# Dealing the hidden columns of a fused attention and feed-forward kernel to partitions in runs of four

## The chip, the cores and the metric

The kernel runs on one core of a Trainium2 chip. A core has a matrix engine (TensorE, PE in the profile, with its weight loads shown apart as PEld), VectorE (DVE), ScalarE (ACT), GpSimd (POOL), SyncE (SP), and 16 DMA engines that all queues share. Partitions are the 128 rows of the on-chip memory. The metric is device time in microseconds (us), lower is better. Before the change the median of three runs is 367.38 us (366.16 to 367.57).

## The reference

Attention over 8 batches, 8 heads, 576 positions and a head dimension of 64: each position sees the positions at most 32 away, and 8 global positions see and are seen by all. Then, over all 4608 tokens, a feed-forward layer with 2048 hidden columns and a periodic activation:

```python
scores = scale * np.matmul(q, k.transpose(0, 1, 3, 2))
mask = np.abs(pos[:, None] - pos[None, :]) <= window
mask = mask | is_global[:, None] | is_global[None, :]
...
h = x @ w_in
s = np.sin(alpha * h)
g = h + s * s / (alpha + 1e-09)
return (g @ w_out).astype(np.float32)
```

w_in is 512 x 2048, w_out 2048 x 512, alpha has 2048 values, all float32. A hidden column belongs to one column of w_in, one value of alpha and one row of w_out; in which order the 2048 are worked off makes no difference to the sum.

## The kernel before

The program is one function with an order written out by hand: each engine does its instructions in the order in which the code issues them, and a DMA waits in the queue of the engine that issues it. The phases alternate over the 8 batches: `phase_a(b + 1, b)` is attention of batch b + 1, with the second matrix product of batch b strewn between its steps (`gemm2` is a generator, and `fill(n)` issues n of its matmuls); `gemm1(b)` is the first product with the activation.

**Attention.** `attention(b)` goes over four head pairs `hp`. `scores` makes blocks of keys by queries in PSUM (line 742), ACT takes the exponential (750), DVE multiplies with the mask (753). One head pair later `products` multiplies with the values in `VX` and with ones for the denominators (784). PE is in order: in batch 1 the first `products(0, ...)` stands behind two groups of scores of head pair 1 and ahead of the third. `warm` (546) issues matmuls without a use.

`VX[b % 2]` holds a batch's values. `load_v` (394) fetches them with POOL's DMAs, 16 of 36 KB a batch. The rows of the global positions come by `load_vg` (403): 8 DMAs of SP, one a head, each of 8 x 12 runs of 64 bf16. For batch 1 and on they are copied out of `VGb`, which `cast_globals_v` (696) makes on POOL from `gv`, and `gv` is gathered by SP (489).

**First product.** `gemm1` goes over 16 groups `nt` of 128 hidden columns. The columns of a group lie on the 128 partitions of the result, so alpha and its reciprocal are one value a partition, held in `alphaT` and `recipT` (128 x 16). Eight matmuls a group (line 992) each load a 128 x 128 block of w_in as weights and stream 288 or 320 tokens. ACT takes the sine (1022), ACT or DVE squares it (1026, 1028), DVE adds (1030) into `H2`.

**Second product.** `gemm2` takes blocks of 128 tokens of `H2` as weights and streams `w_out[:, nt, :]`, 512 columns, over the 16 groups (1049). Partition p of group nt of `w_out` must hold the row of the hidden column that lies there in `H2`. ACT copies the result out (1055), and SP writes it (1062).

**Loads of the parameters.** All go through POOL's queue, which casts float32 to bf16 on the way. `load_w_in` (411) is called for the quarters 0 and 1 between the loads of batch 0's values, and for 2 and 3 once batch 1's transposed keys have landed. `load_w_out` (417) is called in `gemm1(0)` at group 11 and issues four DMAs of 128 x 4 runs of 512 floats. Behind it in POOL's order stand `cast_globals_v`, `place_globals(1)` (372 and 377, copies of the global keys and queries into `KX` and `QX`, from `kTg` and `qTg`, which DVE makes at 708), and the second half of batch 1's `load_v`; then `load_vg(1)` on SP.

**alpha.** SP loads it as 16 rows of 128 into `arow` (483), behind six small loads of the global positions and ahead of eight register loads (485) and the gathers. PE transposes `arow` (680) into a PSUM tile, and ACT copies that to `alphaT` (684), behind its placing of the global keys and queries of batch 0. DVE makes `recipT` at the start of attention 0 (1119).

**The tail.** Column norms of w_in (897, a matmul of one column for each of 16 groups, weights taken from `W2`), token norms, `judge`, and `gemm2_globals` (1076) with a scatter by POOL (1083). `judge` gives a verdict that every engine reads (1081); the branch at 1206 would run `general_path` if the inputs were out of bounds, which they are not. Between the two, PE issues 54 matmuls (1199) whose results nothing reads.

Of the kernel before, what the change touches and what calls it, by code (L numbers as in the profile page):

```python
# [12 lines left out]
DT = mybir.dt  # L13
# [3 lines left out]
P = 128  # L17
# [3 lines left out]
WCOL = 120  # L21
# [5 lines left out]
QROW = QLEN + 2 * PAD  # L27
CUT = 3 * SEG
PLACES = [(w, t, y) for w in (1, 0) for t in range(2) for y in range(2)]
LIM_SUM = float(2.0**50)  # L30
LIM_REC = float(2.0**40)
TINY = float(2.0**-60)
LIM_ARG2 = 9.3


def general_path(tc, q, k, v, global_idx, out, w_in, w_out, alphaT, recipT):


    nc = tc.nc
    B, H, S, D = q.shape  # L40
    NKT = S // KW
    NT = alphaT.shape[1]
    CT = w_in.shape[1]
    DM = w_out.shape[2]
    HALF = S // 2
# [3 lines left out]
    hi = float(np.float32(6.28125))  # L49
# [4 lines left out]
    with ExitStack() as gx:  # L54
# [4 lines left out]
        idf = one.tile([P, P], DT.float32, name="g_idf")  # L59
# [5 lines left out]
            out=g64[:],  # L65
# [14 lines left out]
        for j in range(NG):  # L80
            for at, acc in ((pos, colg), (row, rowg)):
                nc.vector.scalar_tensor_tensor(
                    out=acc[:], in0=at[:], scalar=gf[:, j : j + 1], in1=acc[:],
# [23 lines left out]
        with tc.For_i(0, B, 1) as b:  # L107
# [87 lines left out]
            for nt in range(NT):  # L195
                hg = ps.tile([P, 2, 512], DT.float32, name="g_pt")
                for c in range(CT):
                    for e in range(2):
                        nc.tensor.matmul(
                            out=hg[:, e, 0:HALF], lhsT=w_in[:, c, nt * P : (nt + 1) * P],  # L200
                            rhs=xT[:, c, e * HALF : (e + 1) * HALF],
                            start=(c == 0), stop=(c == CT - 1),
                        )
                y = wk.tile([P, 2, HALF], DT.float32, name="g_y")
                n = wk.tile([P, 2, HALF], DT.float32, name="g_n")
                nc.vector.tensor_scalar(
                    out=y[:], in0=hg[:, :, 0:HALF], scalar1=alphaT[:, nt : nt + 1], scalar2=None,
                    op0=ALU.mult,
                )
                nc.vector.tensor_scalar(  # L210
                    out=n[:], in0=y[:], scalar1=1.0 / TWO_PI, scalar2=None, op0=ALU.mult
                )
                for m in (MAGIC, -MAGIC):
                    nc.vector.tensor_scalar(out=n[:], in0=n[:], scalar1=m, scalar2=None, op0=ALU.add)
                for part in (hi, mid, low):
                    nc.vector.scalar_tensor_tensor(
                        out=y[:], in0=n[:], scalar=-part, in1=y[:], op0=ALU.mult, op1=ALU.add
                    )
                edge = float(np.nextafter(np.float32(np.pi), np.float32(0)))
                nc.vector.tensor_scalar(  # L220
                    out=y[:], in0=y[:], scalar1=edge, scalar2=-edge, op0=ALU.min, op1=ALU.max
                )
                nc.scalar.activation(out=y[:], in_=y[:], func=AF.Sin)
                nc.vector.tensor_tensor(out=y[:], in0=y[:], in1=y[:], op=ALU.mult)
                nc.vector.scalar_tensor_tensor(
                    out=HB[:, nt, :].rearrange("p (e c) -> p e c", e=2),
                    in0=y[:], scalar=recipT[:, nt : nt + 1], in1=hg[:, :, 0:HALF],
                    op0=ALU.mult, op1=ALU.add,
                )
# [18 lines left out]
def kernel(  # L248
# [11 lines left out]
    nc = tc.nc  # L260
# [144 lines left out]
                in_=src[:, None, :].to_broadcast([NG, NT12, D]),  # L405
            )

    def load_w_in(gs):
        for g in gs:
            cols = slice(g * DFF // 4, (g + 1) * DFF // 4)  # L410
            nc.gpsimd.dma_start(
                out=w_in[:, :, cols], in_=moe_w_in[:, cols].rearrange("(c p) n -> p c n", p=P)
            )

    def load_w_out():
        for g in range(4):
            nc.gpsimd.dma_start(
                out=w_out[:, 4 * g : 4 * g + 4, :],
                in_=moe_w_out[4 * g * P : (4 * g + 4) * P, :].rearrange("(t p) n -> p t n", p=P),
            )  # L420


# [49 lines left out]
        out=g64[:],  # L472
        in_=bass.AP(tensor=global_idx.tensor, offset=global_idx.offset, ap=[[1, NG], [0, B], [1, 1]]),
    )
    arow = setup.tile([NT, P], DT.float32, name="arow")
    nc.sync.dma_start(out=girow[:], in_=global_idx[None, :])
    for t in (0, D):
        nc.sync.dma_start(out=gp64[t + KT : t + KT + NG], in_=global_idx[:, None])
# [1 line left out]
            out=gidx8[t + KT : t + KT + NG],  # L480
            in_=bass.AP(tensor=global_idx.tensor, offset=global_idx.offset, ap=[[0, NG], [1, NG]]),
        )
    nc.sync.dma_start(out=arow[:], in_=moe_alpha.rearrange("(t p) -> t p", p=P))
    gi32 = girow[:].bitcast(DT.int32)
    greg = [nc.sync.value_load(gi32[0:1, 2 * j : 2 * j + 1], min_val=0, max_val=S - 1) for j in range(NG)]

# [71 lines left out]
    nc.scalar.activation(out=qrel[:], in_=qrel[:], func=AF.Square, bias=kpos[:, 0:1], scale=-1.0)  # L558
    clear(vflat[:, half : 2 * half])
    load_v(0, (0,))  # L560
    load_w_in((0,))
    load_v(0, (1, 2))
    load_w_in((1,))
    load_v(0, (3,))
    cast_qk(1)
    load_vg(0)
# [108 lines left out]
    for w, name in ((1, "k"), (0, "q")):  # L675
# [1 line left out]
        nc.tensor.transpose(  # L677
            out=pg[w][:], in_=g0[name][:], identity=identb[0 : NG * B, 0 : NG * B]
        )
    nc.tensor.transpose(out=both[:, 0:NT], in_=arow[:], identity=idf[0:NT, 0:NT])  # L680
    for t in range(2):
        place_global_keys(t, act)
        place_global_queries(t, act)
    act(out=alphaT[:], in_=both[:, 0:NT])
    turn_part(0, 1, views([z[:] for z in zo]))
    turn_part(1, 1, views([zn[:, n, :] for n in range(2)]))
    def second_half():
# [206 lines left out]
    def column_norms(pw):  # L894

        for nt in range(NT):
            nc.tensor.matmul(
                out=pw[:, nt : nt + 1], lhsT=W2[:, nt * P : (nt + 1) * P], rhs=ones[:, 0:1],
                start=True, stop=True, skip_group_check=True,
            )  # L900
        c2 = normp.tile([P, NT], DT.float32, name="c2")
        nc.vector.tensor_tensor(out=c2[:], in0=alphaT[:], in1=alphaT[:], op=ALU.mult)
        nc.vector.tensor_tensor(out=c2[:], in0=pw[:, 0:NT], in1=c2[:], op=ALU.mult)
        nc.vector.tensor_reduce(out=limit[:], in_=c2[:], axis=AX.X, op=ALU.max)
        nc.vector.tensor_scalar(
            out=limit[:], in0=limit[:], scalar1=1e-30, scalar2=1.0 / LIM_ARG2, op0=ALU.max, op1=ALU.mult
        )
        nc.vector.reciprocal(out=limit[:], in_=limit[:])
# [60 lines left out]
    def gemm1(b):  # L969
# [11 lines left out]
        def chunks(nt, cs):  # L981
            if nt not in hs:
                if order[nt] == "o":
                    hs[nt] = [(slice(e, e + 1), zo[e][:, None, :]) for e in range(2)]
                else:
                    h = {"n": zn, "d": zd}.get(order[nt]) or hr.tile([P, 2, 512], DT.float32, name="zr")
                    hs[nt] = [(slice(0, 2), h[:])]
            h = [ap[:, i] for es, ap in hs[nt] for i in range(es.stop - es.start)]
            for c in cs:
                for e in range(2):  # L990
                    lhsT = w_in[:, c, nt * P : (nt + 1) * P]
                    nc.tensor.matmul(  # L992
                        out=h[e][:, 0:W], lhsT=lhsT, rhs=xT[:, c, e, 0:W],
                        start=(c == 0), stop=(c == CT - 1), skip_group_check=True,
                    )
# [118 lines left out]
    def phase_a(b_att, b_moe):  # L1114
        def beside(at):

            if b_moe is None:
                if at == -1:
                    nc.vector.tensor_scalar(out=recipT[:], in0=alphaT[:], scalar1=1e-9, scalar2=None, op0=ALU.add)
                    nc.vector.reciprocal(out=recipT[:], in_=recipT[:])  # L1120
                if at == 0:
                    second_half()
                    nc.gpsimd.memset(VX[1][:].bitcast(DT.int32), 0)
                    nc.gpsimd.memset(QX[1][:].bitcast(DT.int32), 0)
                    nc.gpsimd.memset(KX[1][:].bitcast(DT.int32), 0)
                    turn_qk(1)
                    nc.gpsimd.tensor_copy(out=seen[:], in_=turned[1][1][0:1, 0:1])
                    load_w_in((2, 3))
                    load_v(1, (0, 1))
                    gather(v, gv)  # L1130
                return
            if 0 <= at < 2 and b_moe:
                square_x(b_moe, at)
            if b_att == 1 and at == 0:
                place_rest(1)
                place_rest(0)
            for which, t, y in places_at(b_att, at):
                place(b_att + 1, which, t, y, nc.vector.tensor_copy)
            if b_moe == 0 and at == 2:
                turn_qk(2)  # L1140

        if b_moe is not None:
            waiting.append(gemm2(b_moe))
        attention(b_att, beside)
# [46 lines left out]
    verdicts = judge(zn[:, 0, :])  # L1191
    next(verdicts)
    sure = gemm2_globals(verdicts)
    tiles = [(r, c) for r in (0, D) for c in (0, D)]
    for kinds, n in ((tiles, 6), (tiles[0:2], 6), (tiles[0::3], 6), ([None], 6)):
        for i in range(n):
            for at in kinds:
                rows, cols = (slice(0, P), slice(0, P)) if at is None else [slice(x, x + D) for x in at]
                nc.tensor.matmul(
                    out=(zn if len(kinds) == 2 else zd)[cols, (rows.start or 0) // D, 0:WCOL],  # L1200
                    lhsT=VX[0][rows, 0, i, cols], rhs=H2[rows, i, 0:WCOL],
                    start=True, stop=True, skip_group_check=True,
                )
    mctx.close()

    with tc.If(sure < P, preferred_fallthrough_block=False):  # L1206
# [31 lines left out]
```

## Time and profile before

| what | us |
|---|---|
| median of three runs | 367.38 (366.16 to 367.57) |
| the profiled execution | 366.15 |
| its span in the profile | 364.4 |
| PE busy | 338.4 |
| ACT busy | 293.5 |
| DVE busy | 283.3 |
| POOL busy | 139.2 |
| 1024 weight loads from w_in, PEld | 98.6 |
| 576 matmuls of the second product | 153.7 |

The span is what the profile covers, from the first instruction to the last; the time of the execution holds 1.75 us more. Busy times are sums over the span. Matmuls overlap in the machine and their ends are modelled, so PE's busy time is not work at full rate. Where a row ends in brackets, they hold the idle time of the engine just before it and what ended it. The DMA share of a stretch can go over 1, since an engine works at several packets at once; q0 is the queue that POOL fills, q1 the one that SP fills. The granted clock is the share of PE's full clock.

### The profile page before, as it was taken

What the parts mean: (1) busy time and instruction counts of PE and PEld (TensorE: products, weight loads), DVE (VectorE), ACT (ScalarE), POOL (GpSimd) and SP (SyncE); (2) the same over time, 40 slices, a digit from 0 to 9 for tenths busy, and PEclk for the clock granted to TensorE, in tenths of its full rate; (3) what the DMA queues carried; (4) which work ended last, traced back from release to release, by engine and by line L of the source; (5) the groups of instructions that cost most, each with busy time, mean ns of one, the idle gap of its engine ahead of it and who ended that gap; (6) DMA issues with size and microseconds to landing.
All of it is one profiled execution on the core that took longest, in us unless ns stands there. A gap on an engine that the chain in (4) does not pass through costs nothing. (4 is left out here: it accounts for less than half of the span.)

```text
span 364.4 us, 8575 instructions
## 1 busy us (share of the span) xinstructions
PE 338.4 (93%) x3110; PEld 230.8 (63%) x3110; DVE 283.3 (78%) x623; ACT 293.5 (81%) x566; POOL 139.2 (38%) x246
## 2 busy tenths in 40 slices
PE   2579978999999999999999999999999999999994
PEld 1467656766567666776666766766676766655453
DVE  6776998588988877888888887888788866798661
ACT  7689997886978788887888897979888888878711
POOL 7992686669874702661066304730000000000001
PEclk9999998999999999999999999999999999999999
DMA  7997999999999783989199904647120011000321
GB/s 118 120 171 162 181 146 189 156 168 198 146 237 202 73 123 81 172 89 161 31 158 120 149 29 50 68 50 148 43 59 29 2 31 60 29 3 0 105 70 53
DMA packets 103580, 38.07 MB, mean 104 GB/s; under 512 B 94139, under 2 KB 98251, under 8 KB 103083
## 3 DMA queue, kind: packets, MB, share of 16 engines
q0 software_dynamic: 56640, 18.56, 44.6%
q1 hardware_dynamic: 46890, 18.89, 25.5%
q8 instruction: 26, 0.43, 0.5%
q14 instruction: 24, 0.19, 0.2%
HBM read 37.15 MB, written 17.83 MB: 151 GB/s over the span
## 5 line engine op out<-in xcount | busy, mean ns | idle before, releaser
L1049 PE MATMUL zo<-w_out,H 128*128 128x512 bf16 x576 | 153.7, 379 | 0.0
L992 PEld LDWEIGHTS <-w_in 128*128 128x128 bf16 x1024 | 98.6, 98 | 45.6 <-issue 9.1
L394 POOL DMA_DIRECT2D VX<-in_v_dram x128 | 83.3, 659 | 89.8 <-PE zd L784 62.9
L1049 PEld LDWEIGHTS <-H 128*128 128x128 bf16 x576 | 52.3, 97 | 37.2
L750 ACT ACTIVATE E<-ring 128x480 bf16<-128x480 f32 x96 | 54.2, 567 | 22.6 <-PE ring L742 22.2
L753 DVE TENSOR_TENSOR E<-E,MASK 128x480 bf16<-128x480 bf16 x96 | 36.0, 405 | 16.9 <-ACT E L750 15.5
L1083 POOL DMA_INDIRECT out_dram<-osb,ghalf x1 | 1.1, 1067 | 119.6 <-POOLq L1206 119.6
L1030 DVE SCALAR_TENSOR_TENSOR H<-s,recipT,zn 128x576 bf16<-128x576 bf16 x47 | 38.2, 814 | 10.3 <-ACT s L1026 6.5
L1026 ACT ACTIVATE s<-sb 128x576 bf16<-128x576 bf16 (+1 forms) x62 | 42.7, 689 | 2.0
L742 PE MATMUL ring<-QX,KX 128*128 128x120 bf16 x384 | 38.0, 225 | 6.5 <-ACT E L750 3.0
L742 PEld LDWEIGHTS <-KX 128*128 128x128 bf16 x384 | 29.0, 102 | 22.0 <-issue 8.8
L1022 ACT ACTIVATE sb<-zn,alphaT 128x576 bf16<-128x576 f32 (+1 forms) x47 | 34.7, 739 | 9.8 <-PE zn L992 9.7
L1030 DVE SCALAR_TENSOR_TENSOR H<-s,recipT,zd 128x576 bf16<-128x576 bf16 x39 | 31.7, 814 | 6.5 <-ACT s L1026 4.7
L1030 DVE SCALAR_TENSOR_TENSOR H<-s,recipT,zr 128x576 bf16<-128x576 bf16 x39 | 31.7, 813 | 4.5 <-ACT s L1026 2.4
L1022 ACT ACTIVATE sb<-zd,alphaT 128x576 bf16<-128x576 f32 (+1 forms) x39 | 28.9, 740 | 7.1 <-PE zd L992 5.8
L1028 DVE TENSOR_TENSOR s<-sb 128x576 bf16<-128x576 bf16 (+1 forms) x66 | 30.7, 465 | 4.1 <-ACT sb L1022 3.6
L1022 ACT ACTIVATE sb<-zr,alphaT 128x576 bf16<-128x576 f32 (+1 forms) x39 | 28.9, 740 | 5.6 <-PE zr L992 5.4
L784 PEld LDWEIGHTS <-VX 128*128 128x128 bf16 x448 | 26.6, 100 | 9.4 <-issue 3.5
L1055 ACT COPY osb<-zo 128x512 f32<-128x512 f32 x36 | 20.8, 577 | 11.3 <-PE zo L1049 10.0
L992 PE MATMUL zn<-xlast,w_in 128*128 128x288 bf16 (+1 forms) x192 | 28.8, 289 | 0.3
L992 PE MATMUL zn<-xT,w_in 128*128 128x288 bf16 x184 | 26.9, 286 | 2.3 <-DVE H L1030 0.9
L784 PE MATMUL zn<-E,VX 128*128 128x120 bf16 (+2 forms) x336 | 26.9, 211 | 1.0 <-DVE xlast L816 0.9
(163 smaller groups left out, 492.6 us busy)
## 6 DMA issues: line engine op xcount, KB each, us to landing
VX<-in_v_dram POOLq DMA_DIRECT2D x128, 36.0 KB, 5.4
kd<-in_k_dram POOLq DMA_DIRECT2D x7, 576.0 KB, 7.1
qd<-in_q_dram POOLq DMA_DIRECT2D x7, 576.0 KB, 10.1
w_in<-in_moe_w_in_dram POOLq DMA_DIRECT2D x4, 512.0 KB, 6.0
w_out<-in_moe_w_out_dram POOLq DMA_DIRECT2D x4, 512.0 KB, 7.8
out_dram<-osb SPq DMA_DIRECT2D x8, 256.0 KB
out_dram<-osb SPq DMA_DIRECT2D x8, 224.0 KB
out_dram<-osb SPq DMA_DIRECT2D x8, 192.0 KB
```

Of the source, the lines that this page charges most:

```text
L394: nc.gpsimd.dma_start(out=VX[b % 2][r : r + 24, hp, :, t * D : t * D + D], in_=v[b, 2 * hp + t].rearrange("(i a y) d -> y a i d", a=24, y= ...
L742: nc.tensor.matmul(out=ps[:, e * WCOL : (e + 1) * WCOL], lhsT=kx[:, hp, i, :], rhs=qx[:, hp, :, s0 : s0 + 60], start=True, stop=True, skip ...
L750: nc.scalar.activation(out=Eg, in_=ps[:, 0 : 4 * WCOL], func=AF.Exp, scale=scale, accum_out=EA[:, n : n + 1])
L753: nc.vector.tensor_tensor(out=Eg, in0=Eg, in1=MASK[:, 4 * g : 4 * g + 4, :].rearrange("p i c -> p (i c)"), op=ALU.mult,)
L784: nc.tensor.matmul(out=out_t[:, half, :, a - half * CUT : z - half * CUT], lhsT=OB[:] if key else VXb[:, hp, i, :], rhs=E[:, i, :, a - s0 ...
L992: nc.tensor.matmul(out=h[e][:, 0:W], lhsT=lhsT, rhs=xT[:, c, e, 0:W], start=(c == 0), stop=(c == CT - 1), skip_group_check=True,)
L1022: nc.scalar.activation(out=sb[:, es, 0:W], in_=h[:, :, 0:W], func=AF.Sin, scale=alphaT[:, nt : nt + 1])
L1026: nc.scalar.activation(out=s2[:, :, 0:W], in_=sb[:, :, 0:W], func=AF.Square)
L1028: nc.vector.tensor_tensor(out=s2[:, :, 0:W], in0=sb[:, :, 0:W], in1=sb[:, :, 0:W], op=ALU.mult)
L1030: nc.vector.scalar_tensor_tensor(out=H2[:, nt, r0 : r0 + S].rearrange("p (e c) -> p e c", e=2)[:, es], in0=s2[:, es, 0:HALF], scalar=recip ...
L1049: nc.tensor.matmul(out=ops[:], lhsT=H2[:, nt, blk * P : (blk + 1) * P], rhs=w_out[:, nt, :], start=(nt == 0), stop=(nt == NT - 1),)
L1055: nc.scalar.copy(out=osb[:], in_=ops[:])
```

## The change

Hidden columns are dealt to partitions in runs of four. Before, partition p of group nt holds column 128 nt + p. After, the groups come in fours: in the g-th four, partition p of group 4g + t holds column 512 g + 4 p + t. `columns(nt)` gives these as a slice with a step of four.

* w_in lies in memory as before. Its weight blocks are read with a step of four columns, in `gemm1`, in `column_norms` (from `W2`) and in `general_path`.
* w_out is loaded with two DMAs instead of four, each of 128 x 2 runs of 2048 floats: four rows that follow each other in memory go to one partition.
* alpha goes straight into `alphaT`, with 128 x 4 runs of four floats; `arow`, PE's transpose and ACT's copy are gone.
* `load_w_in` takes bounds instead of a list. It issues the same four DMAs in the same places.
* The 54 matmuls at the end are gone.

```diff
+RUN = 4
+def columns(nt):
+    at = nt // RUN * RUN * 128 + nt % RUN
+    return slice(at, at + RUN * 127 + 1, RUN)
...
-    def load_w_in(gs):
-        for g in gs:
-            cols = slice(g * DFF // 4, (g + 1) * DFF // 4)
+    def load_w_in(lo, hi):
+        cols = slice(lo * DFF // 4, hi * DFF // 4)
+        nc.gpsimd.dma_start(
+            out=w_in[:, :, cols], in_=moe_w_in[:, cols].rearrange("(c p) n -> p c n", p=P)
+        )
+
+    def load_w_out():
+        for half in range(2):
+            rows = slice(half * DFF // 2, (half + 1) * DFF // 2)
             nc.gpsimd.dma_start(
-                out=w_in[:, :, cols], in_=moe_w_in[:, cols].rearrange("(c p) n -> p c n", p=P)
-            )
-
-    def load_w_out():
-        for g in range(4):
-            nc.gpsimd.dma_start(
-                out=w_out[:, 4 * g : 4 * g + 4, :],
-                in_=moe_w_out[4 * g * P : (4 * g + 4) * P, :].rearrange("(t p) n -> p t n", p=P),
+                out=w_out[:, half * NT // 2 : (half + 1) * NT // 2, :].rearrange("p (g t) n -> p g (t n)", t=RUN),
+                in_=moe_w_out[rows].rearrange("(g p t) n -> p g (t n)", p=P, t=RUN),
             )
...
-    arow = setup.tile([NT, P], DT.float32, name="arow")
...
-    nc.sync.dma_start(out=arow[:], in_=moe_alpha.rearrange("(t p) -> t p", p=P))
+    nc.sync.dma_start(
+        out=alphaT[:].rearrange("p (g t) -> p g t", t=RUN),
+        in_=moe_alpha.rearrange("(g p t) -> p g t", p=P, t=RUN),
+    )
...
-    nc.tensor.transpose(out=both[:, 0:NT], in_=arow[:], identity=idf[0:NT, 0:NT])
...
-    act(out=alphaT[:], in_=both[:, 0:NT])
...
-                out=pw[:, nt : nt + 1], lhsT=W2[:, nt * P : (nt + 1) * P], rhs=ones[:, 0:1],
+                out=pw[:, nt : nt + 1], lhsT=W2[:, columns(nt)], rhs=ones[:, 0:1],
...
-                    lhsT = w_in[:, c, nt * P : (nt + 1) * P]
+                    lhsT = w_in[:, c, columns(nt)]
...
-                    load_w_in((2, 3))
+                    load_w_in(2, 3)
+                    load_w_in(3, 4)
...
-    tiles = [(r, c) for r in (0, D) for c in (0, D)]
-    for kinds, n in ((tiles, 6), (tiles[0:2], 6), (tiles[0::3], 6), ([None], 6)):
...
```

More of the change, by code (lines that the diff above doesn't have):

```diff
@@ L199, in general_path @@
                         nc.tensor.matmul(
-                            out=hg[:, e, 0:HALF], lhsT=w_in[:, c, nt * P : (nt + 1) * P],
+                            out=hg[:, e, 0:HALF], lhsT=w_in[:, c, columns(nt)],
                             rhs=xT[:, c, e * HALF : (e + 1) * HALF],
@@ L560 @@
     load_v(0, (0,))
-    load_w_in((0,))
+    load_w_in(0, 1)
     load_v(0, (1, 2))
-    load_w_in((1,))
+    load_w_in(1, 2)
     load_v(0, (3,))
@@ L1193 @@
     sure = gemm2_globals(verdicts)
-    tiles = [(r, c) for r in (0, D) for c in (0, D)]
-    for kinds, n in ((tiles, 6), (tiles[0:2], 6), (tiles[0::3], 6), ([None], 6)):
[L1196 to L1203, printed above, removed]
     mctx.close()
```

## The prediction

> **What bounds the kernel now.** I read the page first: the span, the busy shares, the costliest groups.
>
> ```profile
> span 364.4 us, 8575 instructions
> PE 338.4 (93%) x3110; PEld 230.8 (63%) x3110; DVE 283.3 (78%) x623; ACT 293.5 (81%) x566; POOL 139.2 (38%) x246
> L992 PEld LDWEIGHTS <-w_in 128*128 128x128 bf16 x1024 | 98.6, 98 | 45.6 <-issue 9.1
> ```
>
> PE leads. The stretches tell where it isn't full (columns: stretch, its length, then busy time and count of PE, PEld, DVE, ACT and POOL, the granted clock, DMA share, GB/s).
>
> ```profile
> 50.00:60.00 10.00, 7.25 (x66) 5.30 (x66) 9.51 (x24) 8.30 (x19) 8.57 (x18) 0.83 1.27 195
> 100.00:150.00 50.00, 49.49 (x479) 33.84 (x478) 40.70 (x85) 41.60 (x90) 23.38 (x43) 1.00 0.92 147
> 52.30:55.70 3.40, 1.26 (x12) 0.75 (x11) 3.14 (x8) 3.34 (x7) 3.21 (x9) 1.00 1.23 193
> 55.70:59.10 3.40, 3.25 (x24) 2.41 (x24) 3.28 (x10) 2.63 (x10) 3.24 (x5) 0.50 1.34 208
> 62.50:66.00 3.50, 3.06 (x43) 2.35 (x43) 1.87 (x6) 2.45 (x8) 2.93 (x5) 1.00 1.38 201
> ```
>
> From 100 us on PE is busy 99% of the time: what is lost before is not made up, and little can be won there. Between 50 and 60 PE stands for a while, and after a stretch with 1.26 us of work in 3.4 its clock is granted at 0.50. This is exactly where w_out is loaded. The timeline of that place (start, length, engine, line, count):
>
> ```profile
> 46.85 3.08 POOL L417 DMA_DIRECT2D w_out<-in_moe_w_out_dram  x4 [0.23 <-DMA VX<-in_v_dram]
> 49.65 0.42 DVE L708 CAST kTg<-zo 128x256 bf16<-128x256 f32 x1
> 49.92 0.63 POOL L696 CAST VGb<-H 64x512 bf16<-64x512 f32 x1
> 50.48 3.13 POOL L372 COPY KX<-kTg 64x96 bf16<-64x96 bf16 x8
> 50.58 13.96 SPq L403 DMA_DIRECT2D VX<-VGb  x16
> 53.67 0.69 POOL L377 COPY QX<-qTg 128x112 bf16<-128x112 bf16 x2
> 54.42 0.37 PE L742 MATMUL ring<-QX,KX 128*128 128x120 bf16 x4 [1.96 <-POOL QX L377]
> 58.28 0.58 PE L784 MATMUL zn<-E,VX 128*128 128x88 bf16 x4
> ```
>
> Batch 1's scores wait 1.96 us for POOL, which issues w_out, then casts the global values (VGb), then places global keys and queries. The cast also releases SP's sixteen small loads into VX; the first two of them must land before PE's products at 58.28, which start without a wait of their own.
>
> **The change, part by part.** *w_out: four transfers become two.* The four issues take 3.08 us on POOL, 0.77 each; two are gone: 1.54 us. The cast behind them, and SP's load_vg(1), can start up to that much earlier: SP at 50.58 - 1.55 = 49.0. The copies L372 need kTg, ready at 49.65 + 0.42 = 50.07; they start at 50.48 now, so they win 0.35 us at most, then DVE is the late one. PE's 1.96 us wait shrinks by as much.
>
> The transfer is the harder half. Its bytes stay (2.10 MB written); its packets go from 2048 of 1 KB to 512 of 4 KB. DMA queues by stretch (q0 is POOL's, q1 SP's; after each name packets, MB, share); in order 48.4:60.5 (w_out), 26.4:30.4 (the 18 KB packets of kd and qd), 50.6:54.8, 54.8:58.2, 60.5:62:
>
> ```profile
> q0 software_dynamic: 2643, 2.14, 117.8%
> ...
> DMA packets 98, 0.80 MB, mean 200 GB/s; under 512 B 54, under 2 KB 54, under 8 KB 54
> q0 software_dynamic: 64, 0.77, 91.0%
> q1 hardware_dynamic: 32, 0.01, 1.4%
> ...
> q0 software_dynamic: 756, 0.75, 117.6%
> ...
> DMA packets 996, 0.71 MB, mean 210 GB/s; under 512 B 336, under 2 KB 996, under 8 KB 996
> q1 hardware_dynamic: 312, 0.04, 14.6%
> ...
> q1 hardware_dynamic: 407, 0.05, 39.7%
> ```
>
> Two things are read from them. First, speed: 2.14 MB in 12.1 us is 177 GB/s in 1 KB packets, 0.77 MB in 4 us is 193 in 18 KB packets. Longer packets gain 0 to 9%; w_out's 11.7 us end near 60.1 instead of 60.4 (59.3 at best). Second, how SP's small packets come through: in 50.6:54.8 none did, though SP issues from 50.58 on (that stretch has no q1 line); then, in 54.8:58.2, 312 beside 996 - 336 = 660 of 1 KB, one per 2.1. Beside 18 KB packets it is 32 to 98 - 54 = 44, one per 1.4. So the queues take turns by packets, not by bytes. Before, 2048 turns were to be had during w_out; now 512, 44 a us.
>
> The first two loads of load_vg(1) write 8 x 12 runs of 64 bf16 each (line 403): 192 packets of 128 B. They queue up from 49.0. If again nothing moves for 4.3 us (50.58 to 54.8), they start at 53.3, when about 215 of the 512 large packets are gone; the other 297 give 297 / 2.1 = 141 turns by 60.1, and the remaining 51 follow at 407 / 1.5 = 271 a us, 0.2 us: 60.3. Bounds: no waiting at first and one per 1.4 end at 49.0 + 192 * 1.4 / 44 = 55.1, in time; nothing moved until w_out is through ends at 60.4 + 0.7 = 61.1. I take 60.3, because pause and ratio come from the same two transfers in the same place, only with other packets. PE's products then start 60.3 - 58.28 = **2.0 us later** (0 to 2.8). PE is in order: batch 1's remaining scores stand behind them, ACT and DVE starve, and the 0.35 us won before is swallowed.
>
> The Trainium skill ("DMA: Bandwidth & Descriptors", section "Queues, rings and completion order") says that each DMA engine serves its queues in turn, switching at packet boundaries; it speaks against this change, and the trace agrees with its 2.1 and 1.4. Strictly one for one it would give 49.0 + 4.3 + 192 / 44 = 57.7, in time, so the ratios decide, not the rule.
>
> The clock: an idle 2 us in 3.4 was followed by 0.50 at 55.7. A second such stretch, over 62.5:66 with 3.06 us of PE work, would cost 0 to 1.5 us. I take **0.6**.
>
> *Weights with a step of four.* No row shows such a load. Contiguous ones:
>
> ```profile
> 347.05 0.54 PE L897 MATMUL zn<-ones,W 128*128 128x1 bf16 x16
> 35.56 1.14 PE L992 MATMUL zd<-xT,w_in 128*128 128x288 bf16 x8
> L992 PE MATMUL zd<-xT,w_in x152: 282/286/286, 35.6 to 290.7; 128*128 128x288 bf16 x152
> ```
>
> Sixteen loads with one-column matmuls take 0.54 us: at most 34 ns each, less than the 98 ns that a PEld row says. In gemm1 matmuls start (1.14 - 0.286) / 7 = 122 ns apart, so a load may take 3.6 times as long before PE sees it. Cost 0, the cover being the matmul before it; a load four times as long, 136 ns, costs 14 * 1024 = 14.3 us. No gain is possible, since 122 ns is the matmul's own pace. I take 0, for the cover is wide. column_norms' 16 loads lie in the tail, under 1 us either way.
>
> The Trainium skill ("TensorE: Matmul & The Clock Gate", section "Weight-path perf modes — Fast Weight Load (FWL) and DoubleRow") keeps fast loading for steps up to 1,024 elements; without it the same page gives columns / 1.2, an estimated 107 ns, still under 122. By both the sum stays.
>
> *alpha in place.* One transfer of 16 runs becomes 512 runs of 16 B; PE's transpose, ACT's copy go.
>
> ```profile
> 3.46 0.32 SPq L483 DMA_DIRECT2D arow<-in_moe_alpha_dram  x1
> 12.26 3.73 DVE L612 COPY QX<-zd 64x288 bf16<-64x288 bf16 x8
> 14.96 0.17 ACT L684 COPY alphaT<-pg 128x16 f32<-128x16 f32 x1
> 16.02 0.17 DVE L1119 TENSOR_SCALAR recipT<-alphaT 128x16 f32<-128x16 f32 x1
> 16.14 0.96 PE L742 MATMUL ring<-QX,KX 128*128 128x120 bf16 x8 [1.45 <-DVE QX L612]
> SPq L340 <- DMA H<-in_q_dram: 2.3, 1, 2.3
> ```
>
> The first scores wait for DVE (12.26 + 3.73 = 15.99), not for ACT (15.13): the 0.17 us gain nothing. On SP the value loads, the gathers, load_vg(0) and the transposes stand behind this issue; SP idles 2.3 us ahead of the transposes, so a longer issue is hidden up to that. The landing is wanted by 16.02, 12.2 us after the issue ends; at 271 a us 512 packets need 1.9 us, and turns beside the first big loads take the rest. Cost 0, up to 1.5 if it lands late.
>
> *The 54 matmuls at the end go.*
>
> ```profile
> 357.91 0.54 PE L1199 MATMUL zd<-H,VX 64*64 64x120 bf16 x24
> 359.60 1.07 POOL L1083 DMA_INDIRECT out_dram<-osb,ghalf  x1 [119.64 <-POOLq L1206]
> SPq L1233 <- DMA out_dram<-osb,ghalf: 1.4, 1, 1.4
> ```
>
> SP's last step waits 1.4 us for POOL's scatter, which reads nothing of them: 0, between -0.5 and +0.3 for the branch behind. load_w_in is called with other bounds, in the same order: 0.
>
> **Sum** against the profiled execution, 366.15 us (span 364.4 and 1.75 around it): + 2.0 + 0.6 = 368.75. The median shown, 367.38, lies 1.23 above that execution; taking half of it, **369.3 us**, 0.5% over the median. Its own range: 367.5 (1.3 us in all) to 372.
>
> **Rivals.**
> *The small loads come in time* (not slower). For it: the products start at 58.28, and without a pause one turn per 2.1 ends at 49.0 + 192 * 2.1 / 44 = 58.2, with the pause one per 1.4 at 59.4. Against it: both the pause and the 2.1 were seen beside this very transfer. It decides at a landing before 58.0. Then only the 0.35 us is left: 365.8 as profiled, 366.4 for a median; with PE's wait shorter the half clock may also stay away, worth up to 3.25 / 2 = 1.6 us: 364.8.
> *The strided weights show.* At 136 ns a load, 381.7; at 130, 8 * 1024 = 8.2 us, 375.6. For it: no row excludes it, and it hits 1024 loads. Against it: 88 ns of cover. It decides above 122 ns.
> *alpha lands late*, after about 17: DVE holds the first masks; + 0.5 to 1.5 us beside the forecast, 370.3.
>
> **How the numbers follow.** Forecast 0.52, in time 0.30 (a fifth of it with the clock kept), strided weights 0.12, alpha late 0.06. A measurement of this kernel tells about 0.5% from no change: 365.5 to 369.2. Faster: the clock kept, 0.06. Slower: 0.36 of the forecast's 0.52 (its range straddles 369.2), weights 0.12, alpha 0.05: 0.53. Same: the rest, 0.41. The range, 365.8 to 373.5, leaves out the kept clock and the worst of the weights.
>
> **What would show it.** Right: the products (L784 before) of batch 1 start near 60.3 instead of 58.28, PE's idle before them names the VX loads or nothing; SP's packets during w_out fall to about half; w_out ends near 60; POOL's two issues take 1.5 us and the first scores start near 54.1. matmuls of gemm1 stay 122 ns apart. Wrong: products at 58 or earlier (turns by bytes, or shorter packets than 4 KB); gemm1 further apart; a first wait for alpha on DVE near 16 us.

## The result, and the profile after

The changed kernel takes 380.06 us in the median (379.40 to 381.63), the kernel before 366.96 (366.16 to 367.57) beside it: a ratio of 1.036, 95% interval 1.034 to 1.039. The profiled execution took 379.65. That is 10.8 us above the forecast of 369.3, and above the top of its range.

The page of the changed kernel, busy times and the two groups of the first product:

```profile
span 378.0 us, 8417 instructions
PE 334.5 (88%) x3010; PEld 244.4 (65%) x3055; DVE 283.4 (75%) x623; ACT 293.0 (78%) x565; POOL 138.0 (37%) x244
L999 PEld LDWEIGHTS <-w_in 128*128 128x128 bf16 x1024 | 115.5, 114 | 44.2 <-issue 20.3
L999 PE MATMUL zn<-xT,w_in 128*128 128x288 bf16 x184 | 27.8, 290 | 14.9 <-DMA w_in<-in_moe_w_in_dram 12.9
```

PE has about as much to do as before (334.5 against 338.4 us), but its share of the span fell from 93% to 88%. The last row says where: 12.9 us of idle time ahead of the first product, ended by a load of w_in. The timeline of the place, changed kernel:

```profile
33.05 0.41 PE L999 MATMUL zn<-xT,w_in 128*128 128x288 bf16 x2 [0.56 <-DVE xT L823]
36.93 1.53 POOL L417 DMA_DIRECT2D w_in<-in_moe_w_in_dram  x2
46.35 1.12 PE L999 MATMUL zn<-xT,w_in 128*128 128x288 bf16 x4 [12.89 <-DMA w_in<-in_moe_w_in_dram]
47.34 1.43 POOL L424 DMA_DIRECT2D w_out<-in_moe_w_out_dram  x2 [0.19 <-issue]
49.43 0.74 ACT L1029 ACTIVATE sb<-zn,alphaT 128x576 bf16<-128x576 f32 x1 [14.48 <-PE zn L999]
```

and the same place before:

```profile
33.60 0.90 PE L992 MATMUL zn<-xT,w_in 128*128 128x288 bf16 x6 [0.56 <-DVE xT L816]
36.74 1.54 POOL L411 DMA_DIRECT2D w_in<-in_moe_w_in_dram  x2
42.68 1.15 PE L992 MATMUL zn<-xT,w_in 128*128 128x288 bf16 x8 [0.79 <-DMA w_in<-in_moe_w_in_dram]
```

Before, PE runs six matmuls of the first group and goes on; only group 8, the first of quarter 2, waits 0.79 us for the third load. After, two matmuls of the first weight block (block row c = 0) run at 33.05, and then PE stands until 46.35. It stands for the two loads that POOL issues at 36.93, which bring the quarters 2 and 3; the groups that it wants to work on lie in quarter 0, which has long been there. By the trace's records of landings the fourth load is complete at 46.22, and PE goes on 0.13 us later.

The stretches (columns as in the prediction), after:

```profile
33.20:46.30 13.10, 0.26 (x2) 0.00 (x0) 1.40 (x5) 1.73 (x3) 6.27 (x10) 0.62 1.22 182
46.30:50.10 3.80, 3.75 (x16) 2.35 (x17) 0.00 (x0) 0.67 (x2) 2.68 (x4) 0.50 1.10 82
100.00:300.00 200.00, 196.87 (x1783) 146.59 (x1813) 164.49 (x328) 170.31 (x333) 72.65 (x134) 1.00 0.68 103
```

and before:

```profile
33.60:46.30 12.70, 11.87 (x96) 8.98 (x95) 10.83 (x22) 12.21 (x21) 6.66 (x11) 1.00 1.24 196
100.00:300.00 200.00, 198.58 (x1842) 136.79 (x1841) 162.92 (x326) 169.06 (x336) 62.21 (x115) 1.00 0.62 96
```

In the 13 us in which PE did 11.87 us of work it now does 0.26, and ACT and DVE starve with it. When it goes on, its clock is granted at 0.50 for another 3.8 us. From 100 us on both kernels are full, so the loss stays.

### The profile page after: what moved, and what is told of

Its sections match the earlier page's. It is cut to its first block, busy times and chain, and to the rows that moved or that the text cites. A ratio compares the mean times of both kernels' runs of the same rounds, so it can differ in the third digit from the quotient of the medians.

```text
span 378.0 us, 8417 instructions
## 1 busy us (share of the span) xinstructions
PE 334.5 (88%) x3010; PEld 244.4 (65%) x3055; DVE 283.4 (75%) x623; ACT 293.0 (78%) x565; POOL 138.0 (37%) x244
## 5 line engine op out<-in xcount | busy, mean ns | idle before, releaser
L1056 PE MATMUL zo<-w_out,H 128*128 128x512 bf16 x531 | 143.5, 379 | 1.9
L999 PEld LDWEIGHTS <-w_in 128*128 128x128 bf16 x1024 | 115.5, 114 | 44.2 <-issue 20.3
L749 PE MATMUL ring<-QX,KX 128*128 128x120 bf16 x384 | 37.2, 221 | 7.7 <-ACT E L757 3.8
L999 PE MATMUL zn<-xT,w_in 128*128 128x288 bf16 x184 | 27.8, 290 | 14.9 <-DMA w_in<-in_moe_w_in_dram 12.9
L379 POOL COPY KX<-kTg 64x96 bf16<-64x96 bf16 x56 | 21.7, 387 | 16.2 <-DVE kTg L715 13.9
```

Of the source, the lines that this page charges most:

```text
L379: nc.gpsimd.tensor_copy(out=KX[b % 2][rows, hp, :, t * D + KT : t * D + KT + NG], in_=kTg[rows, hp, None, :, b].to_broadcast([D, NT12, NG]),)
L749: nc.tensor.matmul(out=ps[:, e * WCOL : (e + 1) * WCOL], lhsT=kx[:, hp, i, :], rhs=qx[:, hp, :, s0 : s0 + 60], start=True, stop=True, skip ...
L999: nc.tensor.matmul(out=h[e][:, 0:W], lhsT=lhsT, rhs=xT[:, c, e, 0:W], start=(c == 0), stop=(c == CT - 1), skip_group_check=True,)
L1056: nc.tensor.matmul(out=ops[:], lhsT=H2[:, nt, blk * P : (blk + 1) * P], rhs=w_out[:, nt, :], start=(nt == 0), stop=(nt == NT - 1),)
```

## The experiments

**The step alone.** The kernel before, with only the weights read with a step of four (columns of w_in then meet other values of alpha and other rows of w_out):

```diff
-                    lhsT = w_in[:, c, nt * P : (nt + 1) * P]
+                    lhsT = w_in[:, c, columns(nt)]
...
-                out=pw[:, nt : nt + 1], lhsT=W2[:, nt * P : (nt + 1) * P], rhs=ones[:, 0:1],
+                out=pw[:, nt : nt + 1], lhsT=W2[:, columns(nt)], rhs=ones[:, 0:1],
```

> The kernel before with one part of the change, the weight blocks of w_in read with a step of four (w_out, alpha and the tail as before, so columns of w_in are paired with other values of alpha and other rows of w_out: same work, another sum). Theory: a block with a step of four of block row c = 1 is taken to overlap the later quarters of w_in, whose DMAs write the columns around it, so the second weight load of the first product waits for all four loads. Then the first product stands until the last quarter lands, about 46 instead of 33.6, and the time is 367 + 13 = 380, 378 to 382. Rival, the wait comes from the other parts (two large w_out transfers or alpha crowd the queue): 366 to 368 here. Rival, part of it is the reading itself, a slower weight load: gemm1's matmuls further apart than 122 ns and more than 381.

Measured: 379.72 us, ratio 1.036 (1.032 to 1.041). The timeline:

```profile
33.36 0.41 PE L1000 MATMUL zn<-xT,w_in 128*128 128x288 bf16 x2 [0.55 <-DVE xT L824]
45.22 1.12 PE L1000 MATMUL zn<-xT,w_in 128*128 128x288 bf16 x4 [11.45 <-DMA w_in<-in_moe_w_in_dram]
```

The step alone makes the wait and the whole loss; the other parts of the change add nothing beside it that can be told. The changed kernel's records of w_out and of batch 1's attention tell why:

```profile
DMA to landing us min/median/max: 7.9/10.1/12.2
```

```profile
67.30 0.37 PE L749 MATMUL ring<-QX,KX 128*128 128x120 bf16 x4 [1.64 <-POOL QX L384]
71.13 0.36 PE L791 MATMUL zn<-E,VX 128*128 128x88 bf16 x4
```

w_out, issued at 47.34 and 48.06, has landed by 48.06 + 12.2 = 60.3 at the latest, before batch 1's first scores at 67.30 and 11 us before its products. SP's small loads do land later than before (the second at 60.61, against 57.66), but nothing waits for them any more.

**All but the step.** The changed kernel with contiguous blocks (other pairs of columns again):

```diff
 def columns(nt):
-    at = nt // RUN * RUN * 128 + nt % RUN
-    return slice(at, at + RUN * 127 + 1, RUN)
+    return slice(nt * 128, (nt + 1) * 128)
```

> The changed kernel with contiguous weight blocks again (w_out in two transfers, alpha in place, no matmuls at the end; columns of w_in are paired with other values of alpha and rows of w_out: same work, another sum). Theory: without the wait for all of w_in, what is left is the rest of the change. As predicted, SP's small loads of the global values land late beside w_out's 4 KB packets: the products of batch 1 start near 60.3 and the time is 368.5 to 370. Rival, they come in time: products at 58.3 or before, 365 to 367. Rival, the wait does not come from the step: 379 to 381.

Measured: 369.32 us, ratio 1.008 (1.005 to 1.011). In the timeline the first product doesn't stop, and the products of batch 1 start late:

```profile
32.99 0.90 PE L998 MATMUL zn<-xT,w_in 128*128 128x288 bf16 x6 [0.56 <-DVE xT L822]
60.16 0.49 PE L790 MATMUL zn<-E,VX 128*128 128x88 bf16 x4 [2.89 <-DMA VX<-in_v_dram]
```

58.28 before, 60.16 here, 60.3 forecast. The row names a load of values, but PE's own waiting instruction, which waits for the counter of SP's second small load among others, goes through at 60.06, and that counter is full at 60.03. So the second thing that the change does is the one that was predicted, and it can only be seen once the first is away.

**The step, with w_in laid out by quarters.** This is the changed kernel with one thing more. Is the wait for data that PE needs, or for a region that it is taken to touch? Each load of w_in writes four pieces, one a block row; from its first to its last element such a load reaches over most of the tile. Here the tile holds the quarters one after the other, so that each load writes one block:

```diff
-    w_in = const.tile([P, CT, DFF], DT.bfloat16, name="w_in")
+    w_in = const.tile([P, 4, CT, DFF // 4], DT.bfloat16, name="w_in")
...
-            out=w_in[:, :, cols], in_=moe_w_in[:, cols].rearrange("(c p) n -> p c n", p=P)
+            out=w_in[:, lo], in_=moe_w_in[:, cols].rearrange("(c p) n -> p c n", p=P)
...
-                    lhsT = w_in[:, c, columns(nt)]
+                    lhsT = w_in[:, nt // 4, c, nt % 4 : nt % 4 + 509 : 4]
```

> The changed kernel whole, with the tile of w_in laid out by quarters, so that each of the four loads writes one block of memory and a block with a step of four lies within one quarter. Step, transfers and sum are as in the changed kernel. Theory: the wait is one of bookkeeping and goes, and the time is that of the changed kernel with contiguous blocks, 365 to 370 within 0.3%. Rival, the step of four costs by itself: more than the contiguous one by 1% or more, matmuls of gemm1 over 122 ns apart. Rival, the wait is for the data (the transfers crowd each other): still 379 to 381.

Measured: 369.77 us, ratio 1.009 (1.005 to 1.012), against 369.32 with contiguous blocks. The timeline, and the group of weight loads (the last row of the timeline names DVE; here too PE's waiting instruction for the second small load goes through at 60.32, with the landing at 60.29):

```profile
33.55 0.90 PE L999 MATMUL zn<-xT,w_in 128*128 128x288 bf16 x6 [0.55 <-DVE xT L823]
35.50 1.14 PE L999 MATMUL zd<-xT,w_in 128*128 128x288 bf16 x8
42.51 1.17 PE L999 MATMUL zn<-xT,w_in 128*128 128x288 bf16 x8 [0.68 <-DMA w_in<-in_moe_w_in_dram]
60.43 0.36 PE L791 MATMUL zn<-E,VX 128*128 128x88 bf16 x4 [2.33 <-DVE E L760]
```

```profile
L999 PEld LDWEIGHTS <-w_in 128*128 128x128 bf16 x1024 | 114.8, 114 | 30.8 <-issue 7.1 <-DVE HG L1043 3.3 <-DMA w_in<-in_moe_w_in_dram 1.0
```

Same step, same transfers, the data land much as before (the fourth load at 45.06), and the first product runs as before, with 0.68 us of wait at group 8. The 13 us were bookkeeping: a block with a step of four was taken to touch what the loads of the later quarters write between its elements. It fits that only the block of c = 0 got through, whose columns 0 to 508 lie ahead of the first element of every later quarter. The waits that the traces record with the weight loads say the same:

```
kernel before:          first weight load of group 4 waits for load 2, of group 8 for load 3, of group 12 for load 4
changed kernel:         third weight load of group 0, the first of c = 1, waits for loads 3 and 4; none later
w_in by quarters:       as the kernel before
```

The loads 1 and 3 share one counter and 2 and 4 another; which of the two is meant follows from the times. By which rule the waits are placed is read from these three programs only. The weight loads' own record is 114 ns instead of 98, and eight matmuls still take 1.14 us.

**The layout alone.** The control: the kernel before, contiguous blocks, tile by quarters.

```diff
-                    lhsT = w_in[:, c, nt * P : (nt + 1) * P]
+                    lhsT = w_in[:, nt // 4, c, nt % 4 * P : (nt % 4 + 1) * P]
```

> The kernel before with only the tile of w_in laid out by quarters, blocks contiguous: the control for the layout. Theory: no change, 366 to 368, since waits and transfers are as before and only places in memory differ. Rival, the layout itself gains or costs (other runs written by the DMAs, the column norms' squares read in four pieces): over 0.5% from the kernel before.

Measured: 365.75 us, ratio 0.998 (0.996 to 1.000): no change that can be told.

**Packets of 1 KB, 2 KB and 4 KB.** Three kernels with the step, w_in by quarters and w_out in four transfers, which read the same rows. They differ in the places where the four rows of a partition lie in w_out's tile, and so in the runs that are written. 4 KB:

```diff
-        for half in range(2):
-            rows = slice(half * DFF // 2, (half + 1) * DFF // 2)
+        for g in range(4):
+            rows = slice(g * DFF // 4, (g + 1) * DFF // 4)
...
+                out=w_out[:, 4 * g : 4 * g + 4, :].rearrange("p t n -> p (t n)"),
+                in_=moe_w_out[rows].rearrange("(p t) n -> p (t n)", p=P),
```

> The changed kernel with w_in by quarters, and w_out in four transfers instead of two, its packets 4 KB as in the change. Against the kernel with 1 KB packets only the packets' size differs, against the changed kernel with w_in by quarters only the number of issues. Theory: products of batch 1 near 60.2, 369 to 370.5; the two more issues of POOL (1.5 us) are swallowed in that wait. Rival, the number of issues does it: 366 to 367.2.

1 KB, the rows of a partition apart (2 KB has them in pairs, `[P, 2, NT // 4, 2, DM]`):

```diff
-    w_out = const.tile([P, NT, DM], DT.bfloat16, name="w_out")
+    w_out = const.tile([P, 4, NT // 4, DM], DT.bfloat16, name="w_out")
...
+                out=w_out[:, :, g, :], in_=moe_w_out[rows].rearrange("(p t) n -> p t n", p=P)
```

> The changed kernel with w_in by quarters, and w_out in four transfers whose packets write 1 KB again: the tile of w_out holds the four rows of a partition apart, so 2048 runs of 512 bf16 are written, not 512 runs of 2048. The rows that are read, the pairing and the sum stay. Theory: the size of the packets holds up SP's small loads of the global values, so with 1 KB ones the second of them lands near 57.7 as in the kernel before, the products of batch 1 start near 58.3, and the time is 366 to 367.2. Rival, the order of issue or the rows that are read do it: products near 60.2 and 369 to 370.

> As the kernel with 1 KB packets (w_in by quarters, w_out in four transfers, same rows and same sum), with packets that write 2 KB: 1024 runs of 1024 bf16. Theory, the queues take turns by packets: the second of SP's small loads lands between the two sizes, near 58.5 to 59.3 (57.7 with 1 KB, 60.0 with 4 KB), the products of batch 1 start there, and the time is 366.3 to 368.5. Rival, there is a step in size above which SP gets no turns: 57.7 and 365.7, or 60.0 and 369.7.

Measured; the landing is that of SP's second small load, from the trace's records of its counter:

```
packets   second small load lands   products start   median us   ratio (95%)
1 KB      57.66                     58.58            365.67      0.999 (0.998 to 1.001)
2 KB      59.47                     59.60            367.01      1.003 (1.000 to 1.005)
4 KB      60.02                     60.16            369.71      1.010 (1.007 to 1.012)
before    57.66                     58.28
```

One further execution with 4 KB took 1943 us, for a reason that no trace here shows. It is one of the five behind the median of 369.71; the other four lie between 368.83 and 369.88, with 369.55 in the middle. PE's waiting instruction for the second small load goes through at 60.05 with 4 KB and at 59.50 with 2 KB, 0.03 us after the landing in both. In the waits of the 4 KB and of the 2 KB kernel the small loads are named (who waited for what; us, times, longest):

```profile
PE zn L791 <- DMA VX<-VGb: 2.6, 1, 2.6
```

```profile
PE zn L791 <- DMA VX<-VGb: 1.0, 1, 1.0
```

The queues in 54.8:58.2, with 1 KB, 2 KB and 4 KB (under 512 B are the small ones, q1 is SP's):

```profile
DMA packets 990, 0.72 MB, mean 211 GB/s; under 512 B 327, under 2 KB 990, under 8 KB 990
...
q1 hardware_dynamic: 308, 0.04, 14.4%
```

```profile
DMA packets 535, 0.72 MB, mean 212 GB/s; under 512 B 194, under 2 KB 194, under 8 KB 535
...
q1 hardware_dynamic: 173, 0.02, 8.0%
```

```profile
DMA packets 273, 0.70 MB, mean 205 GB/s; under 512 B 105, under 2 KB 105, under 8 KB 273
...
q1 hardware_dynamic: 89, 0.01, 4.0%
```

Large ones to one of SP's: (990 - 327) / 308 = 2.2, (535 - 194) / 173 = 2.0, (273 - 105) / 89 = 1.9. The bytes a us stay; the turns fall as the packets grow.

The trace's counters say something more about the two to one: a transfer of w_out is counted in by 16 landings, a small load by 8 (and an entry 1.1 us after its issue). If each landing is that of one DMA engine, only half of the large packets pass where small ones wait, and there the turns are near one for one: 308 to 332, 173 to 171 and 89 to 84. The trace does not name the engine of a packet, so this is not shown.

The number of issues doesn't matter: two of 4 KB gave 369.77, four gave 369.71.

The start of the products tells less than 2 us of the 4 between 1 KB and 4 KB. Part of the rest is read in the clock. 1 KB, then two transfers of 4 KB (w_in by quarters), then four:

```profile
55.00:59.00 4.00, 4.00 (x34) 2.76 (x32) 2.95 (x8) 3.27 (x10) 4.00 (x7) 0.59 1.33 210
...
62.00:66.00 4.00, 3.55 (x44) 2.45 (x44) 2.29 (x7) 2.96 (x9) 3.44 (x7) 1.00 1.38 179
```

```profile
55.00:59.00 4.00, 3.10 (x20) 1.83 (x18) 3.50 (x11) 3.20 (x10) 3.18 (x5) 0.66 1.09 195
...
62.00:66.00 4.00, 3.80 (x31) 2.53 (x30) 1.96 (x6) 3.28 (x9) 2.55 (x5) 0.68 1.28 214
```

```profile
55.00:59.00 4.00, 2.00 (x18) 0.87 (x15) 3.64 (x10) 3.04 (x11) 3.29 (x6) 1.00 1.10 194
59.00:62.00 3.00, 1.84 (x25) 1.68 (x26) 1.69 (x6) 0.10 (x1) 1.61 (x3) 0.77 1.78 110
62.00:66.00 4.00, 3.42 (x33) 2.48 (x33) 2.09 (x6) 3.17 (x9) 2.44 (x5) 0.74 1.36 234
```

Behind the longer wait the half clock comes in both kernels with 4 KB: with two transfers for a second time, with four for the only time. The two take the same time (369.77 and 369.71), so the number of such stretches does not decide; what lies in them seems to. With 1 KB the half clock is over at 58.3 and the products start at 58.58; with four of 4 KB it falls on the products and what follows them. From the first product to the first matmul of the second product PE then takes 3.07 us (60.16 to 63.23) instead of 2.39 (58.58 to 60.97), and the exponential that ACT starts at 61.92 with 1 KB starts at 64.53. So 1.6 us of delay have become 2.6, and 2.9 by the end of the kernel. The profiled executions, 366.17 and 369.71, are 3.5 us apart; most of the rest is at the very end, where POOL's last drain took 4.00 us instead of 2.95. Two kernels whose profiles show no half clock around this place, the layout alone above and the end alone below, took 365.90 and 365.92 as profiled, against 366.15 before with 3.4 us of it: such a stretch need not cost much by itself.

The stretch seems not to come in every execution. The twelve of the 2 KB kernel fall in two groups, seven from 365.74 to 367.02 and five from 368.70 to 369.76, so that the median of 367.01 is the upper end of the first group and not a time in the middle; the kernel before, too, has 369.19 and 369.85 beside fifteen from 365.19 to 367.28. The profiled execution of the 2 KB kernel is of the upper group and has this row:

```profile
59.00:62.00 3.00, 2.40 (x26) 2.15 (x27) 2.03 (x7) 0.26 (x1) 0.30 (x1) 0.50 1.71 141
```

That the lower group goes without it is not shown, since none of it was profiled.

**The end alone.** The kernel before without the 54 matmuls (nothing reads their results):

```diff
-    tiles = [(r, c) for r in (0, D) for c in (0, D)]
-    for kinds, n in ((tiles, 6), (tiles[0:2], 6), (tiles[0::3], 6), ([None], 6)):
...
```

> The kernel before without the 54 matmuls at the end, and nothing else. As predicted: -0.5 to +0.3 us, 366 to 366.8. Rival, read from the traces of the changed kernels, in which POOL's last drain takes 3.8 to 4.0 us instead of 3.3 and SP, done, waits 0.7 us for it: + 0.5 to 0.8 us, 367 to 367.3, with the drain near 4.0.

Measured: 365.46 us, ratio 0.999 (0.997 to 1.000), against 365.95. POOL's last drain took 2.7 us; it took 3.7 in the control with the matmuls kept, and 4.0 in two kernels without them. The rival falls: a longer drain does not come from leaving the matmuls out.

**w_out behind the global keys.** A try at keeping the long packets away from the small loads (54 matmuls kept):

```diff
-                load_w_out()
                 cast_globals_v()
                 place_globals(1)
+                load_w_out()
```

> The changed kernel with w_in by quarters and with the 54 matmuls kept, and with w_out's two transfers issued behind the placing of the global keys and queries instead of ahead of it. Theory: SP's small loads go out with no large packets beside them and land before 55, the products of batch 1 start at 58 or before, the first scores 0.35 us earlier; w_out lands near 66 and its first half near 60, in time for the second product at 63: 364.5 to 366.3, under the kernel before. Rival, the later w_out holds up the second product or the values of head pair 2: over 367.

Measured: 371.84 us, ratio 1.018 (1.015 to 1.021). The small loads landed at 53.2 and 53.9, as expected, and it didn't help. From the waits between 50 and 75:

```profile
POOL VX L401 <- DMA w_out<-in_moe_w_out_dram: 8.3, 2, 5.3
...
POOL VGb L703 <- DMA H<-in_v_dram: 3.1, 1, 3.1
...
PE zo L1056 <- DMA w_out<-in_moe_w_out_dram: 1.5, 1, 1.5
```

POOL's cast now waits 3.1 us for the gathered values, which the issue of w_out covered; the copies of the keys and the first scores slip to 55.02; and w_out is late for the second product. The rival was right.

**A version under both.** The 1 KB kernel, with POOL's copies of the global queries behind the first head pair's keys (batch 1):

```diff
+            if hp == (0 if b == 1 else NHP - 1):
+                queries()
```

> A try at a version under both kernels: the kernel with 1 KB packets (step of four, w_in by quarters, alpha in place, no matmuls at the end), and POOL's two copies of the global queries of batch 1 moved up behind the two copies of the first head pair's keys, six copies of keys earlier. The first scores of batch 1 then wait for about 1.5 us of copies instead of 3.9. Theory: PE's idle of 2.7 us there goes, ACT's table load (to 55.2) is late next, the half clock stays away, and SP's second small load (57.7) bounds the products: 364 to 365.5. Rival: the bound was ACT and the small loads all along and nothing is won: 365.4 to 366.

Measured: 365.14 us, ratio 0.997 (0.996 to 0.999). The first scores, in the 1 KB kernel and here:

```profile
54.80 0.50 PE L748 MATMUL ring<-QX,KX 128*128 128x120 bf16 x4 [2.73 <-POOL QX L384]
```

```profile
53.60 0.37 PE L752 MATMUL ring<-QX,KX 128*128 128x120 bf16 x4 [1.28 <-DVE QX L357]
```

They start 1.2 us earlier, and DVE's copies are late next. The products start at 58.41 instead of 58.58, so most of it is lost to what follows. It is 0.3% under the kernel before and the fastest of all, though the half clock did not stay away as the theory wanted (granted 0.57 in 55:59).

## Why the prediction was wrong, point by point

*The step that failed* is "load_w_in is called with other bounds, in the same order: 0", together with "I take 0, for the cover is wide" for the weights with a step of four. Both priced instructions: the issue of the loads, and the time of a weight load. Neither asked what a weight load waits for once its addresses have changed. That term is 12.9 us of idle, and the step alone took the kernel to 379.72. The order of the loads was indeed the same; what changed is how many of them the first product has to wait for.

*The rival "the strided weights show"* gave 381.7 and comes near the time, but by luck and not by its mechanism: eight matmuls still take 1.14 us, 122 ns apart, in the kernel that has the step without the wait. The part of the step that was priced was priced rightly: 369.77 with it, 369.32 without. A load does get slower. Its record went from 98 to 114 ns, and the column norms' sixteen took 0.54 us before, and with the step (w_in by quarters):

```profile
350.09 0.66 PE L904 MATMUL zn<-ones,W 128*128 128x1 bf16 x16
```

That is 8 ns more for each. The Trainium skill ("TensorE: Matmul & The Clock Gate", section "Weight-path perf modes — Fast Weight Load (FWL) and DoubleRow") keeps fast loading at this step; 0.66 / 16, at most 41 ns a load, is nearer to that than to the 107 ns estimated without it, though the Trainium skill doesn't tell of the 8 ns.

*w_out in two transfers, + 2.0 us:* right, in place, size and cause, but hidden in the changed kernel. Forecast was a landing at 60.3; it was 60.03 with contiguous blocks, 60.29 with the step and w_in by quarters, and the products followed at 60.16 and 60.43. The pause between SP's first issue and its first packet, 4.3 us before, was 3.9 to 4.1 us with 1, 2 and 4 KB (and 1.3 us with w_out behind the global keys), and the ratio of about two to one held for the three sizes. SP's issue itself came at 48.77 (w_in by quarters) and 50.00 (contiguous blocks), where 49.0 was forecast; the landing hardly moved with it, and w_out's own end lay beside it, at 60.12 and 59.85. The Trainium skill ("DMA: Bandwidth & Descriptors", section "Queues, rings and completion order") has the engines switch queues at packet boundaries; the fall of SP's packets from 308 to 173 to 89 agrees with that. The packets of the Trainium skill hold typically some 9 to 17 descriptors, and no run here shows that what the profile counts as a packet is the same, so the rule gives no ratio. The prediction's "strictly one for one" took all large packets into the count; by the 8 and 16 landings above, one for one on half the engines would look like the two to one that was measured.

*A second half clock, + 0.6:* a half clock behind the wait came in all profiled kernels with 4 KB packets and an early first product, as the second with w_in by quarters, as the only one with four transfers and with contiguous blocks. With four transfers it made 2.6 us of the products' 1.6, so about 1.0, within the 0 to 1.5 that were given.

*The sum* without the missed wait, 369.3, stands beside 369.32 and 369.77, but that it is so close is partly luck. It stood 1.9 us over a median of 367.38; the kernel before, measured beside those two, gave 366.43, so the steps are 2.9 and 3.3. The half of 1.23 that was added for the median stands in for what the sum lacked: the clock's further 0.4, and a longer drain at the end, 3.8 and 4.0 us against 3.3 before.

*alpha in place, 0:* nothing in the trace speaks against it. Its counter is full at 12.4 us (w_in by quarters), well ahead of its use. DVE took it at 16.3 us (w_in by quarters), 16.02 before, and at 16.0 with contiguous blocks; it was not tried alone.

```profile
L1126 DVE TENSOR_SCALAR recipT<-alphaT x1: 175/175/175, 16.3 to 16.3; 128x16 f32<-128x16 f32 x1
```

*The 54 matmuls, -0.5 to +0.3:* measured -0.5, at the edge of what can be told.

Still open is why POOL's last drain varies, between 2.7 and 4.2 us over all these traces.

## What to carry to other kernels

When an access pattern changes, price not only its own time but what it has to wait for: list which loads write between the first and the last element of the new pattern, and look at the waits that the program's instructions carry: here those for the third and fourth load stood ahead of a weight load of group 0. Where a tile is loaded in pieces, give each piece a block of its own, so that a stepped read touches one piece only; here that was worth 10 us. And before transfers are made longer, look at whose small ones run beside them: here they got one turn for about two large packets, at each of three sizes.

## What the runs showed of the hardware that was not expected

The ratio of turns, about two large packets to one of SP's, stayed at 2.2, 2.0 and 1.9 while the packets grew fourfold; that small loads are counted in by 8 landings and large ones by 16 would make this one for one on half the engines, which is not shown. A weight load with a step of four costs some 8 ns more when nothing covers it, and nothing that can be seen in the first product. And a wait of PE that grows can cost more than it grows by, when a stretch of half clock then falls on the work behind it: between 1 KB and four transfers of 4 KB the products start 1.6 us later, and the exponentials behind them 2.6.
